# Attention values as the stationary operand, two heads on the two halves of the partitions, and router logits from rows not yet divided

## The chip, the cores and the metric

One core of a Trainium2 chip runs the whole kernel. The metric is device time in microseconds (us) of one execution, as the median of several runs. A smaller time is better.

## What is computed

Three stages follow each other. First a windowed attention over 4 batches, 8 heads, 576 positions and 64 values per head; each query sees itself and the 127 keys before it, with a bias that falls with the distance. Then a router sends each of the 2304 rows of 512 values to one of 8 experts. Last a gated layer with 1536 hidden units.

```python
scores = np.where(mask, scale * q @ k.T + bias, -1e9)      # mask: 0 <= query - key < 128
attn = exp(scores - max); attn = attn / (sum(attn) + 1e-9)
x = (attn @ v)                       # rows of 8 heads x 64 = 512 values
logits = x @ w_gate + modality_bias[modality_id]; e_idx = argmax(logits)
out = gate_w * (relu(x @ w1[e_idx]) @ w2[e_idx])
xn = out / rms * rms_g;  g = xn @ w_gate2;  return (g * sigmoid(g) * (xn @ w_val)) @ w_out
```

## The kernel before

The program is written in an order by hand: a list `AT` gives, for each half step n, the order of the routines and the lag of each. A query tile t has 128 rows; g = 0 and 1 are its two groups of four heads, so a tile has two half steps, and there are 18 tiles. A routine with lag L works in half step n on the pair (t, g) with 2t + g = n - L. Routines that work once for a tile run when g is 0. Each engine works through its own instructions in that order.

For one tile the routines are these. `tq`, `tk` turn the query and key rows on TensorE (bank "d", two buffers), and `qhi`, `khi` copy the result out on ScalarE. `qk` makes the scores (lag -1). It has queries stationary, 64 rows deep, and keys moving; the heads j = 0 and 1 of a pair lie on the two halves of the partitions. `ttr0`, `ttr1` add the bias on VectorE and find the largest. `exp0`, `exp1` make the exponentials on ScalarE with their sums. In the first six tiles `mix` and `pprev` fold the two key blocks on GpSimd. `pt` turns the weights on TensorE, `pall` (ScalarE) and `pcur` (VectorE) copy them out. `pv` (lag 2) multiplies by the values: the turned weights, 128 x 128, are stationary and 64 values of one head move, and the result in bank "c" (one buffer) has queries on partitions. A product of 32-bit operands appears as two LDWEIGHTS and two MATMUL records.

`xs` (lag 3, VectorE) divides that result by the sums and writes the row tile which is later sent away. `tx` (lag 4, TensorE) turns the row, `xhi` (lag 5, ScalarE) copies it out, `lg` (lag 6) multiplies by the 512 x 8 router weights into the bank "few", four products that accumulate into 8 columns. `gate` (lag 7, VectorE) adds the modality bias and finds the best expert, `gexp`, `rk` and `route` (lag 8) make the gate and the place of the row within its expert, and `place` (lag 9) sends the row to DRAM.

The bank "few" is one tile that also takes the counts of `rk` and the small turns of `mscale`. The latter makes a power of two from the largest of the weights, in five parts: part 0 on VectorE, part 1 a turn on TensorE (L598), part 2 on VectorE, part 3 two small products on TensorE (L603), part 4 on VectorE (L606 to L612). `SCALE` says in which half steps they start. Parts 1 and 3 stand ahead of `pt` of the next and the next but one half step, parts 2 and 4 at these half steps' ends.

While attention runs, the expert weights of the two experts chosen early are loaded (`weights`, on the SyncE queue with the loads of q, k and v and with the fills of DRAM) and split into high and low halves (`wsplits`, on ScalarE, GpSimd and VectorE, `SPLIT` pieces in a half step, and two a half step after the last entry of `SPLIT`). From half step 36 on, each half step ends with an eighth of the first expert product (`gemm1`), and after half step 44 `gemm2` follows, which needs all split pieces and their scaled copies (L637). All that comes later, from some 245 us on, is not touched.

Of the kernel before, what the change touches and what calls it, by code (L numbers as in the profile page):

```python
# [8 lines left out]
F32 = mybir.dt.float32  # L9
# [41 lines left out]
SPLIT = {**{n: 1 for n in range(25, 33)}, **{n: 2 for n in range(33, 37)}}  # L51
SCALE = {22: (0, 1), 25: (1, 2), 31: (2, 3), 36: (3, 4)}
# [31 lines left out]
def attn_moe_glu(tc, I, out, dbg=None):  # L84
    nc = tc.nc
    with contextlib.ExitStack() as top:
# [77 lines left out]
        wgn = tail.tile([P, KD, E], F32, name="wgn", bufs=1)  # L164
# [169 lines left out]
        def pv(t, g):  # L334
            full, oc, op = geo(t)[0], geo(t)[4], geo(t)[5]
            if g == 0:
                X[t] = bank("c", "xp").rearrange("p (h d) -> p h d", h=H)
            pa, pc = G.pop((t, g))[2:]
            for j in range(2):
                for u in range(2):  # L340
                    h = 4 * g + 2 * u + j
                    if mixed(t):
                        cur, prev = pc[:, j, u], pa[:, j, u]
                    else:
                        cur, prev = (pa, pc)[j][:, u, oc // P], (pa, pc)[j][:, u, op // P]
                    nc.tensor.matmul(X[t][:, h], cur, T["v", t][:, h], start=True, stop=not full)  # L346
                    if full:
                        nc.tensor.matmul(X[t][:, h], prev, T["v", t - 1][:, h], start=False, stop=True)  # L348
# [6 lines left out]
        def rs(t):  # L355
            r = small([P, H], F32, "rs")
# [4 lines left out]
        def xs(t):  # L361
            x = t1.tile([P, XW], F32, name=f"xs{t}") if t <= T0 else row_tile("xs")
            nc.vector.tensor_tensor(
                x[:, :D].rearrange("p (h d) -> p h d", h=H), X[t], M.pop(t)[:, :, None].to_broadcast([P, H, DH]), ALU.mult
            )
            X[t] = x

        def tx(t):
            x = bank("d", "tx")
            for k in range(KD):  # L370
                nc.tensor.transpose(x[:, k * P : k * P + P], X[t][:, k * P : k * P + P], ident)
            M[t] = x.rearrange("p (k x) -> p k x", k=KD)

        def xhi(t):
            x = block_tile("xT").rearrange("p (k x) -> p k x", k=KD)
            nc.scalar.activation(x, M[t], AF.Copy)
            M[t] = x

        def lg(t):
            x = M.pop(t)  # L380
            for k in range(KD):
                nc.tensor.matmul(few[:, P : P + E], x[:, k], wgn[:, k], start=k == 0, stop=k == KD - 1)  # L382
# [1253 lines left out]
```

## Time and profile before

| what | value |
| --- | --- |
| median of 3 runs | 866.93 us (861.96 to 879.2) |
| the profiled execution, its own time | 858.8 us |
| its span, first to last instruction | 857.1 us |
| attention, from the first turn of queries to the end of the last first-layer product | 4.8 to 224.4 us |
| mean granted clock of TensorE over the span | 0.975 of full speed |

The profile is of one execution. A matmul's recorded duration holds the time that its result needs to come out, so the distance from one start to the next tells more than the duration. Stretches named "tile" below run from the first query turn of one tile to that of the next.

### The profile page before, as it was taken

The page shows a single profiled execution, that of the slowest core. Times are in us where ns is not written, and L with a number is a line of the kernel's source. Part 1 is how long each engine was busy: PE and PEld are TensorE (multiplying, and loading weights), DVE is VectorE, ACT ScalarE, POOL GpSimd, SP SyncE. Part 2 cuts the span into 40 slices and gives each one's busy share as a digit, 9 for nine tenths or more (in the row PEclk, how much of TensorE's full clock was granted, in tenths as well). Part 3 has the DMA queues.
Part 4 walks back from the last instruction along what each step waited for, and adds up shares of the span by engine and source line. Part 5 has one row for each costly group of instructions (what it writes and reads, how often), then busy time and mean ns, then how long its engine had stood idle before and what let it go on. Part 6 is the DMA issues. An engine that isn't in the chain of part 4 may idle for free.

```text
span 857.1 us, 17524 instructions
## 1 busy us (share of the span) xinstructions
PE 815.1 (95%) x5826; PEld 560.2 (65%) x5826; DVE 610.2 (71%) x1685; ACT 433.9 (51%) x992; POOL 201.1 (23%) x259
## 2 busy tenths in 40 slices
PE   8999998989799999999999999899999999999994
PEld 6889787876345544444455555468787787888882
DVE  8778787875984578997676657667666676667752
ACT  6877777974544566774455433242333233233221
POOL 3552113575632234565100010000001001001001
PEclk9999997998899999999999999999999999999998
DMA  9974995652165655794652046001001000001001
GB/s 181 215 177 134 307 235 159 174 173 91 71 177 180 193 186 161 256 304 146 244 206 103 1 152 241 1 25 51 13 2 62 14 1 38 1 2 39 2 2 39
DMA packets 100473, 101.99 MB, mean 119 GB/s; under 512 B 63136, under 2 KB 75424, under 8 KB 100384
## 3 DMA queue, kind: packets, MB, share of 16 engines
q1 hardware_dynamic: 92848, 86.34, 35.0%
q0 software_dynamic: 4400, 14.20, 4.4%
q8 instruction: 53, 0.87, 0.4%
q10 hardware_dynamic: 3136, 0.30, 0.3%
q14 instruction: 36, 0.29, 0.1%
HBM read 67.18 MB, written 33.89 MB: 118 GB/s over the span
## 4 chain that ended last, share of the span: by engine, by line
issue 42%; PE 36%; DVE 10%; DMA 5%; ACT 4%; POOL 2%; SPq 0%; POOLq 0%; DVEq 0%; ACTq 0%
PE y L840 6%; PE h L807 6%; PE g L1184 4%; PE s L242 3%; PE xp L346 3%; PE xp L348 3%; PE pt L311 2%; PE acc L1359 2%; PE h L794 2%; DVE pb L270 1%; DMA raw<-gd 1%; ACT pb L281 1%; PE few L382 1%; DVE wr L777 1%; POOL out L863 1%
## 5 line engine op out<-in xcount | busy, mean ns | idle before, releaser
L1184 PE MATMUL g<-xc,gv 128*128 128x192 f16 x1680 | 146.7, 247 | 0.0
L1184 PEld LDWEIGHTS <-gv 128*128 128x128 f16 x1680 | 139.8, 98 | 9.3
L863 POOL DMA_INDIRECT out<-o,ix x18 | 17.8, 991 | 400.4 <-ACT o L1368 397.7
L840 PE MATMUL y<-W,wr 128*128 x304 | 91.9, 384 | 2.0 <-DVE fi L855 2.0
L840 PEld LDWEIGHTS <-wr 128*128 128x128 f16 x456 | 45.0, 99 | 61.6 <-issue 10.6
L1359 PE MATMUL acc<-go,alo 128*128 128x512 f16 x216 | 82.5, 382 | 0.0
L281 ACT ACTIVATE pb<-pb,mn 128x256 f32<-128x256 f32 (+4 forms) x160 | 74.5, 468 | 10.0 <-DVE mn L270 9.2
L1200 PE MATMUL gv<-xn,gv 128*128 128x384 f16 x432 | 75.1, 329 | 1.1 <-DVE one L1326 0.7
L1359 PEld LDWEIGHTS <-ahi 128*128 128x128 f16 x432 | 41.5, 98 | 41.6 <-issue 3.9
L807 PEld LDWEIGHTS <-W 128*128 x384 | 37.7, 99 | 44.4 <-issue 2.6
L1359 PE MATMUL acc<-go,ahi 128*128 128x512 f16 x216 | 64.3, 380 | 0.7 <-ACT ahi L1320 0.7
L897 POOL TENSOR_TENSOR cw<-cw,cv 128x512 int32<-128x512 int32 x36 | 50.2, 1394 | 62.9 <-issue 14.2
L840 PE MATMUL y<-wr,wr 128*128 x152 | 58.4, 384 | 5.4 <-DVE wr L637 5.4
L1200 PEld LDWEIGHTS <-gv 128*128 128x128 f16 x432 | 42.5, 98 | 31.9 <-issue 2.8
L270 DVE CUSTOM_DVE_ANT_0 pb<-s,bias 128x256 f32<-128x256 f32 (+4 forms) x160 | 53.5, 379 | 13.6 <-PE s L242 12.1
L807 PE MATMUL h<-xhi,W 128*128 128x512 f16 x192 | 59.3, 379 | 0.0
L1325 ACT ACTIVATE one<-one,undo 128x384 f32<-128x384 f32 x24 | 14.8, 615 | 83.1 <-DVE one L1316 83.1
L1359 PE MATMUL acc<-gv,ahi 128*128 128x512 f16 x180 | 54.2, 383 | 0.7 <-ACT ahi L1320 0.7
L1320 ACT ACTIVATE ahi<-one 128x384 f16<-128x384 f32 x36 | 18.8, 523 | 56.8 <-DVE one L1326 56.8
L242 PE MATMUL s<-kT,qT 64*128 64x256 f32 (+1 forms) x288 | 42.1, 403 | 0.6 <-DVE mn L270 0.4
L1316 DVE TENSOR_TENSOR u<-g,u 128x384 f32<-128x384 f32 x48 | 26.6, 555 | 17.0 <-PE g L1184 17.0
L1320 ACT ACTIVATE ahi<-other 128x384 f16<-128x384 f32 x36 | 18.8, 523 | 39.2 <-DVE other L1326 39.2
(331 smaller groups left out, 1768.0 us busy)
## 6 DMA issues: line engine op xcount, KB each, us to landing
raw<-gd SPq DMA_DIRECT2D x20, 768.0 KB, 4.5
gd<-cw SPq DMA_DIRECT2D x36, 256.0 KB, 3.3
wr<-in_moe_w SPq DMA_DIRECT2D x16, 512.0 KB, 6.0
cv<-in_moe_w_gate SPq DMA_DIRECT2D x12, 512.0 KB, 4.7
cv<-in_moe_w_val SPq DMA_DIRECT2D x12, 512.0 KB, 5.7
cv<-in_moe_w_out SPq DMA_DIRECT2D x12, 512.0 KB, 4.8
xd<-zrow SPq DMA_DIRECT2D x20, 257.0 KB, 4.9
xg<-xd SPq DMA_DIRECT2D x19, 257.0 KB, 3.2
```

Source lines behind the costliest of these rows:

```text
L242: nc.tensor.matmul(sps[j][:, u, :W], qT[rows, i], win(i, j), start=True, stop=True)
L270: nc.vector.tensor_tensor_reduce(pb[rw, u, x0:x1], sp[rw, u, x0:x1], bias[rw, h, b0 + x0 : b0 + x1], 1.0, 3.0e38, ALU.add, ALU.min, M[t][0 ...
L281: nc.scalar.activation(pb[rw, u, x0:x1], pb[rw, u, x0:x1], AF.Exp, bias=mn[rw, h : h + 1], scale=-1.0, accum_out=sm[rw, h : h + 1],)
L807: nc.tensor.matmul(hp, WH[0][k // 2][:, ds(w, 1), part, k % 2, q * P : q * P + P], x[:, k], start=k == 0 and n == 0, stop=k == KD - 1 and ...
L840: nc.tensor.matmul(y, x[:, k, cols], r, start=k == 0 and i == 0, stop=k == KF - 1 and i == 2)
L863: return nc.gpsimd.indirect_dma_start(dst[:, :], bass.IndirectOffsetOnAxis(ap=ix[:, 0:1], axis=0), src, None, bounds_check=NTOK - 1, oob_i ...
L897: nc.gpsimd.tensor_tensor(ci, ci, low.bitcast(I32), ALU.add)
L1184: nc.tensor.matmul(acc[:, gv * HT : gv * HT + HT], GV[p][:, a, gv, i, m * P : m * P + P], XC[c][:, b, j, m], start=m == 0 and n == 0, stop ...
L1200: nc.tensor.matmul(acc[:, :CHT], w[:, m * P : m * P + P], XC[c][b][:, k], start=k == 0 and n == 0, stop=k == KD - 1 and n == 2,)
L1316: add = lambda out, x, y: nc.vector.tensor_tensor(out, x, y, ALU.add)
L1320: nc.scalar.activation(ahi, si, AF.Copy, scale=2.0**-LOW)
L1359: nc.tensor.matmul(acc, a[:, cols], GO[f][part], start=f == 0 and n == 0, stop=f == NFF - 1 and n == 2,)
```

## The change

`pv` has the values (128 keys x 64) stationary and the turned weights (128 keys x 128 queries) moving. Heads j = 0 and 1 write to partitions 0 to 63 and 64 to 127 of the same columns, and their products alternate. The result has the 512 values on partitions and the queries along the columns. So `xhi` (now lag 4) copies it first, `tx` (lag 4, at the half step's end) turns it back into rows, and `lg` (lag 5) takes the undivided copy: for each k it multiplies by a 128 x 16 router block, two heads side by side with zeros in between, and writes 16 columns of its own, 64 in all. `xs` (lag 5) divides the turned rows. `gate` (lag 6) multiplies the 64 logits by 1/sum, adds over the heads (two VectorE instructions more), and goes on as before. Everything behind it has a lag smaller by one. `mscale` has all of its parts at the ends of half steps, `SCALE` and `SPLIT` start one half step earlier but for the last scale step, and the fills of DRAM come three instead of two in half steps 10 and 11, since they end one half step sooner.

```diff
-SPLIT = {**{n: 1 for n in range(25, 33)}, **{n: 2 for n in range(33, 37)}}
-SCALE = {22: (0, 1), 25: (1, 2), 31: (2, 3), 36: (3, 4)}
+SPLIT = {**{n: 1 for n in range(24, 32)}, **{n: 2 for n in range(32, 36)}}
+SCALE = {21: (0, 1), 24: (1, 2), 30: (2, 3), 36: (3, 4)}
...
-        wgn = tail.tile([P, KD, E], F32, name="wgn", bufs=1)
+        wgn = tail.tile([P, KD, 2 * E], F32, name="wgn", bufs=1)
...
-                X[t] = bank("c", "xp").rearrange("p (h d) -> p h d", h=H)
+                X[t] = bank("c", "xp").rearrange("p (k x) -> p k x", k=KD)
             pa, pc = G.pop((t, g))[2:]
-            for j in range(2):
-                for u in range(2):
-                    h = 4 * g + 2 * u + j
...
-                    nc.tensor.matmul(X[t][:, h], cur, T["v", t][:, h], start=True, stop=not full)
-                    if full:
-                        nc.tensor.matmul(X[t][:, h], prev, T["v", t - 1][:, h], start=False, stop=True)
+            for u in range(2):
+                for n in range(1 + full):
+                    for j in range(2):
+                        if mixed(t):
+                            p = (pc, pa)[n][:, j, u]
+                        else:
+                            p = (pa, pc)[j][:, u, (oc, op)[n] // P]
+                        i = 2 * g + u
+                        nc.tensor.matmul(
+                            X[t][DH * j : DH * j + DH, i], T["v", t - n][:, 2 * i + j], p, start=n == 0, stop=n == full
+                        )
...
+        def xhi(t):
+            x = block_tile("xT").rearrange("p (k x) -> p k x", k=KD)
+            nc.scalar.activation(x, X[t], AF.Copy)
+            X[t] = x
+
+        def tx(t):
+            x = bank("d", "tx")
+            for k in range(KD):
+                nc.tensor.transpose(x[:, k * P : k * P + P], X[t][:, k], ident)
+            X[t] = x, X[t]
+
+        def lg(t):
+            x = X[t][1]
+            for k in range(KD):
+                nc.tensor.matmul(few[:, P + 2 * E * k : P + 2 * E * (k + 1)], x[:, k], wgn[:, k], start=True, stop=True)
...
-            nc.vector.tensor_tensor_reduce(l, few[:, P : P + E], mbt, 1.0, 3.0e38, ALU.add, ALU.min, s[:, 0:1])
+            y = small([P, H, E], F32, "lh", 1)
+            nc.vector.tensor_tensor(
+                y, few[:, P : P + H * E].rearrange("p (h e) -> p h e", h=H),
+                M.pop(t)[:, :, None].to_broadcast([P, H, E]), ALU.mult,
+            )
+            nc.vector.tensor_reduce(l, y.rearrange("p h e -> p e h"), AX.X, ALU.add)
+            nc.vector.tensor_tensor_reduce(l, l, mbt, 1.0, 3.0e38, ALU.add, ALU.min, s[:, 0:1])
...
-            nc.scalar.activation(wgn, wg, AF.Copy, scale=-1.0)
+            nc.vector.memset(wgn, 0.0)
+            for j in range(2):
+                x = slice(DH * j, DH * j + DH)
+                nc.scalar.activation(wgn[x, :, E * j : E * j + E], wg[x], AF.Copy, scale=-1.0)
...
-            ("tq", -2), ("mix1", 1), ("gexp", 8), ("qhi", -2), ("rk", 8), ("xhi", 5), ("khi", -1), ("ttr0", 0),
-            ("ttr1", 0), ("lg", 6), ("ws", -1), ("exp0", 0), ("route", 8), ("weights", 11),
-            ("mix0", 0), ("tx", 4), ("pt", 1), ("pall", 1), ("exp1", 0), 
-            ("gate", 7), ("rs", 2), ("pv", 2), ("pprev", 1), ("qk", -1), ("xs", 3), ("vm", 1), ("place", 9), ("tk", -2),
+            ("tq", -2), ("mix1", 1), ("xhi", 4), ("gexp", 7), ("qhi", -2), ("rk", 7), ("khi", -1), ("ttr0", 0),
+            ("ttr1", 0), ("lg", 5), ("ws", -1), ("exp0", 0), ("route", 7), ("weights", 10), ("mix0", 0),
+            ("pt", 1), ("pall", 1), ("exp1", 0), ("gate", 6), ("rs", 2), ("pv", 2), ("pprev", 1),
+            ("qk", -1), ("xs", 5), ("vm", 1), ("place", 8), ("tk", -2), ("tx", 4),
             ("pcur", 1), ("wm", -1),
...
-                for x, r, w in fills[:2]:
+                m = 3 if 9 < n < FILL else 2
+                for x, r, w in fills[:m]:
...
-                if name == "pt":
-                    for x in (1, 2):
-                        if n - x in SCALE:
-                            mscale(*SCALE[n - x], 2 * x - 1)
...
-            for x, half in ((0, 0), (1, 2), (2, 4)):
+            for x, half in ((0, 0), (1, 1), (1, 2), (2, 3), (2, 4)):
                 if n - x in SCALE:
                     mscale(*SCALE[n - x], half)
```

## Rows read from the trace of the kernel before

**Rows 1.** The page's first part: busy us, share of the span, instructions, by engine.

```profile
PE 815.1 (95%) x5826; PEld 560.2 (65%) x5826; DVE 610.2 (71%) x1685; ACT 433.9 (51%) x992; POOL 201.1 (23%) x259
```

**Rows 2.** Stretches by tile: length, busy us by engine, granted clock, DMA share, GB/s.

```profile
core 0: us, PE busy (x) PEld busy (x) DVE busy (x) ACT busy (x) POOL busy (x), PEclk, DMA share, GB/s
...
27.80:36.70 8.90, 8.90 (x78) 8.04 (x76) 6.38 (x28) 6.84 (x22) 5.04 (x7) 1.00 0.94 214
36.70:47.00 10.30, 9.33 (x81) 8.17 (x79) 9.24 (x47) 9.42 (x32) 5.85 (x10) 1.00 0.77 197
...
66.40:76.40 10.00, 10.00 (x89) 9.05 (x87) 8.39 (x42) 7.64 (x27) 2.54 (x4) 1.00 0.52 132
76.40:85.90 9.50, 9.50 (x89) 8.86 (x87) 7.05 (x38) 6.80 (x23) 2.79 (x5) 1.00 0.50 145
...
95.00:106.90 11.90, 10.27 (x69) 8.26 (x67) 8.82 (x36) 8.13 (x28) 1.16 (x2) 0.86 1.07 298
...
128.60:145.80 17.20, 14.81 (x91) 12.81 (x90) 11.99 (x54) 11.84 (x38) 6.47 (x12) 0.70 0.47 135
145.80:156.40 10.60, 10.13 (x89) 9.07 (x87) 8.09 (x39) 10.50 (x36) 5.27 (x8) 1.00 0.67 179
156.40:166.30 9.90, 9.90 (x89) 9.01 (x87) 8.89 (x45) 8.84 (x28) 4.92 (x6) 1.00 0.69 187
...
188.00:201.40 13.40, 11.16 (x52) 8.68 (x51) 7.00 (x18) 5.13 (x13) 7.32 (x11) 0.62 0.06 21
...
224.40:234.40 10.00, 4.64 (x14) 1.65 (x13) 9.93 (x21) 3.64 (x7) 7.63 (x7) 0.66 0.07 27
```

**Rows 3.** Timeline of TensorE's matmuls over one half step: start, length, line, count.

```profile
152.60 1.04 PE L311 MATMUL pt<-ident,pb 128*128 128x128 f32 x8
153.47 0.33 PE L346 MATMUL xp<-vn,pa 128*128 128x64 f32 x2
...
154.76 0.39 PE L346 MATMUL xp<-vn,pc 128*128 128x64 f32 x2
154.98 0.39 PE L348 MATMUL xp<-vn,pc 128*128 128x64 f32 x2
155.30 1.14 PE L242 MATMUL s<-kT,qT 64*128 64x256 f32 x8
156.36 0.66 PE L187 MATMUL tq<-ident,qn 128*128 128x128 f32 x4
```

**Rows 4.** Lines L348 and L598, weight loads and matmuls: ns min/median/max, starts, shape.

```profile
L348 PEld LDWEIGHTS xp<-vn,pa x168: 191/193/334, 21.2 to 202.1; 128*128 128x128 f32 x168
L348 PE MATMUL xp<-vn,pa x168: 274/275/422, 21.3 to 202.2; 128*128 128x64 f32 x168
...
L598 PEld LDWEIGHTS few<-ident,mam x4: 79/80/84, 113.1 to 201.1; 128*1 128x1 f32 x4
```

**Rows 5.** Timeline of two engines around a scale step.

```profile
130.07 0.63 PE L371 MATMUL tx<-ident,xs 128*128 128x128 f32 x4
...
132.86 0.17 DVE L420 TENSOR_TENSOR ranks<-few,ranks 128x16 f32<-128x16 f32 x1
...
133.09 0.37 PE L598 MATMUL few<-ident,mam 128*1 128x128 f32 x1 [2.39 <-DVE ranks L420]
```

**Rows 6.** Who waited for whom, 0 to 220 us: total us, times, longest.

```profile
DVE xs L363 <- PE xp L348: 10.3, 12, 1.2
...
DVE l L389 <- PE few L598: 6.5, 1, 6.5
...
DVE vmax L351 <- DMA vn<-in_v: 2.5, 1, 2.5
```

**Rows 7.** VectorE's instructions by line, 76.4 to 85.9 us: busy us, mean ns.

```profile
L351 DVE TENSOR_REDUCE vmax<-vn 128x1 f32<-128x512 f32 x1 | 0.7, 677 | 0.0
...
L420 DVE TENSOR_TENSOR ranks<-few,ranks 128x16 f32<-128x16 f32 x1 | 0.2, 155 | 0.0
```

**Rows 8.** Timeline of TensorE where the second expert product starts.

```profile
230.35 0.59 PE L840 MATMUL y<-wr,wr 128*128 x1 [5.36 <-DVE wr L637]
```

More of the change, by code (lines that the diff above doesn't have):

```diff
@@ L336, in pv @@
             if g == 0:
-                X[t] = bank("c", "xp").rearrange("p (h d) -> p h d", h=H)
+                X[t] = bank("c", "xp").rearrange("p (k x) -> p k x", k=KD)
             pa, pc = G.pop((t, g))[2:]
-            for j in range(2):
-                for u in range(2):
-                    h = 4 * g + 2 * u + j
[L342 to L345, printed above, removed]
-                    nc.tensor.matmul(X[t][:, h], cur, T["v", t][:, h], start=True, stop=not full)
-                    if full:
-                        nc.tensor.matmul(X[t][:, h], prev, T["v", t - 1][:, h], start=False, stop=True)
+            for u in range(2):
[9 more added lines that the diff above has]
+                        )
         def vm(t):
@@ L355, in rs @@
         def rs(t):
-            r = small([P, H], F32, "rs")
+            r = small([P, H], F32, "rs", 3)
             nc.vector.tensor_scalar(r, M.pop(t)[1], 1e-9, None, ALU.add)
@@ L359, in rs @@
             M[t] = r
[L361 to L365, printed above, removed]
+        def xhi(t):
+            x = block_tile("xT").rearrange("p (k x) -> p k x", k=KD)
+            nc.scalar.activation(x, X[t], AF.Copy)
             X[t] = x
@@ L370, in tx, with xs @@
             for k in range(KD):
[L371 to L377, printed above, removed]
+                nc.tensor.transpose(x[:, k * P : k * P + P], X[t][:, k], ident)
+            X[t] = x, X[t]
         def lg(t):
-            x = M.pop(t)
+            x = X[t][1]
             for k in range(KD):
-                nc.tensor.matmul(few[:, P : P + E], x[:, k], wgn[:, k], start=k == 0, stop=k == KD - 1)
+                nc.tensor.matmul(few[:, P + 2 * E * k : P + 2 * E * (k + 1)], x[:, k], wgn[:, k], start=True, stop=True)
+        def xs(t):
+            x = t1.tile([P, XW], F32, name=f"xs{t}") if t <= T0 else row_tile("xs")
+            nc.vector.tensor_tensor(
+                x[:, :D].rearrange("p (h d) -> p h d", h=H), X[t][0].rearrange("p (h d) -> p h d", h=H),
+                M[t][:, :, None].to_broadcast([P, H, DH]), ALU.mult,
+            )
+            X[t] = x
         def gate(t):
@@ L388, in gate @@
             mbt = MB[:, t] if t < NT - 2 else MBL[:, t - NT + 2]
-            nc.vector.tensor_tensor_reduce(l, few[:, P : P + E], mbt, 1.0, 3.0e38, ALU.add, ALU.min, s[:, 0:1])
+            y = small([P, H, E], F32, "lh", 1)
+            nc.vector.tensor_tensor(
+                y, few[:, P : P + H * E].rearrange("p (h e) -> p h e", h=H),
+                M.pop(t)[:, :, None].to_broadcast([P, H, E]), ALU.mult,
+            )
+            nc.vector.tensor_reduce(l, y.rearrange("p h e -> p e h"), AX.X, ALU.add)
+            nc.vector.tensor_tensor_reduce(l, l, mbt, 1.0, 3.0e38, ALU.add, ALU.min, s[:, 0:1])
             k8 = small([P, E], F32, "k8")
@@ L948, in attention_step @@
             if 3 <= n < 2 * T0 + LAG["route"] + 1 or n >= FILL:
-                for x, r, w in fills[:2]:
+                m = 3 if 9 < n < FILL else 2
+                for x, r, w in fills[:m]:
                     nc.sync.dma_start(x[r : r + P], (EX[1] if EX else zrow)[:, :w])
-                fills = fills[2:]
+                fills = fills[m:]
+                assert n < FILL - 1 or all(x is yd for x, _, _ in fills)
             for name, lag in AT:
```

## The prediction

> **What bounds the kernel now.** I read the page's totals first. TensorE is busy for 815.1 of 857.1 us and VectorE for 610.2 [rows 1], but such shares mix stages, so I cut the attention at each tile's first query turn [rows 2]. The reader is to compare, in each row, TensorE's busy time with the length and then with the next busiest engine. From 66.40 to 76.40 and from 76.40 to 85.90 TensorE is busy without a break, and VectorE has 8.39 and 7.05 us of work. Here TensorE sets the pace. In the tile from 36.70 TensorE has 9.33, ScalarE 9.42 and VectorE 9.24 of 10.30 us, so relief of one alone gives little. In the one from 145.80 ScalarE fills 10.50 of 10.60. From 95.00 on the DMA engines are full (1.07) and VectorE waits 2.5 us for a load of values [rows 6]. The tile from 128.60 takes 17.20 us at a mean clock of 0.70. The nine other stretches of attention repeat these patterns; their numbers are in the sum below as gains only.
>
> Then the timeline, for what a half step costs on TensorE [rows 3]. Two records of `pv` start every 154.98 - 154.76 = 0.22 us, so one takes 0.11 us, although only 64 columns move. A load of the 128 columns of weights stands before each. That the load is the limit is read from the neighbour: eight turns of 128 columns take 153.47 - 152.60 = 0.87 us, 0.11 each, with twice the moving columns. A full half step has 16 such records: 16 x 0.112 = 1.79 us. From the last pair of `pv` to `qk` it is 155.30 - 154.98 = 0.32 instead of 0.22: 0.1 us is lost on the change to products 64 rows deep. `qk` takes 156.36 - 155.30 = 1.06 us for four pairs of records.
>
> Last the waits. At 133.09 the turn of a scale step had idled TensorE for 2.39 us until `route` (L420) had read the bank "few" at 132.86 [rows 5]. After it the clock is at 1.2 instead of 2.4 GHz for most of the tile [rows 2]. A later scale step keeps VectorE from `gate` (L389) for 6.5 us [rows 6].
>
> **The change part by part.** *`pv`.* The 16 records remain, but each streams 128 columns from a 64-column load, and two heads use different halves of the array's columns. No row shows two column halves. The nearest row is `qk`, whose heads use two halves of the array's rows: four pairs of 256 columns in 1.06 us, of which 0.2 goes to entering and leaving, so (1.06 - 0.2) / 4 = 0.215 us for a pair, 0.108 for a pair of 128 columns [rows 3]. If the column halves run side by side as these row halves do, a half step has 8 pairs x 0.11 = 0.88 us. If they take turns it is 16 x 0.11 = 1.76. I take the first, since `qk` is the same pattern of 32-bit products with j alternating. The loads go on under the stream: a 128-column load lasts 191 ns, a one-column load 79 [rows 4], so a 64-column load lies between, and now the load of 128 columns fits into each 0.11 us.
>
> The Trainium skill, page "TensorEngine Tiling (Array Packing)", section "When to Use Tiling", recommends just this swap with two column tiles when 64 columns move, up to twice as fast; the trace before has no such product, so no row confirms it.
>
> One more change of the array's shape per half step, from turns to `pv`, costs 0.1 to enter and 0.1 for the first load that nothing covers, 0.2 us by the same rows (bounds: nothing, if the change into `qk` replaces it, and 0.4). So a full half step of TensorE saves 1.79 - 0.88 - 0.2 = 0.71 us, a tile 1.4. Over 32 full and 4 short half steps (0.25 each) that is 23.7 us if nothing else were in the way.
>
> *What the records meet.* `gate` grows by a product and a sum of 64 elements on VectorE. A 16-element operation takes 155 ns and a 512-element reduction 677 [rows 7]; two of 64 lie between 0.3 and 1.4 us, and I take 0.45, near the first, per tile. It gives something back: `xs` waited 10.3 us in 12 tiles for `pv` of its own half step [rows 6], and now reads a turn made in the half step before. `xhi` stands near the head of ScalarE's half step, before `gexp`, `qhi`, `khi` and the exponentials, and waits for `pv` of the half step before. `pv` ends a whole `qk`, 1.06 us, before that half step does, so I cost the wait at nothing; without that cover ScalarE would lose up to 1 us a tile. `tx` moves from the middle of TensorE's half step to its end, ahead of nothing that is due; it needs `xhi`, 0.6 us into the half step. `lg` moves 16 columns instead of 8 under the same loads: nothing. The second copy and the clearing of the router block are once and early: nothing, below 1 us with no cover. On SyncE the third fill (257 KB) stands before loads in two half steps; at the 197 to 214 GB/s of that stretch [rows 2] it is 1.3 us of DMA, which the loads' lead covers.
>
> So a tile's new length is the largest of TensorE less 1.4, VectorE plus 0.45 and ScalarE, with 0.3 for waits that don't overlap. The tile from 66.40 goes from 10.0 to 9.0, the one from 76.40 from 9.5 to 8.4. With the two beside them (one held by VectorE) I count 3.2 us. The tile from 27.80 has its DMA engines at 0.94, so it can't fall below 8.4, a gain of 0.5; the one before it 0.3, the one from 36.70 0.4, the next 0.7. The tile from 95.00 gains nothing and the next 0.2, since the weights' loads fill the DMA engines. The tile from 145.80 gains nothing (ScalarE), the one from 156.40 goes to 8.89 + 0.45 + 0.3, a gain of 0.3, the last one 1.3. The two stretches around the first product (from 176.4 and 201.4) gain 0.7 each for their `pv`. Together 8.3.
>
> *The scale steps.* At a half step's end the turn's read of "few" lies a whole half step behind, so the 2.39 us go. VectorE's part 2 now waits at the half step's end for part 1, which lies behind `qk`. What is queued behind it is `ttr0`, which needs that `qk` anyway. In the tile from 128.60 the stall goes and so should the slow clock: a mean of 0.70 over 17.2 us means 10.3 us at half speed, 5.1 us of loss. I count 2.4 + 4.9 = 7.3 there, and 1.2 for the smaller stalls at 117 to 128.6.
>
> *The end of attention.* From 188.00 to 201.40 the clock averages 0.62 [rows 2], 10.2 us at half speed or 5.1 lost. Fewer waits may keep it up; I count half, 2.5, and 0.7 for `pv`. At 230.35 TensorE had idled 5.36 us for the last scaled copies of the second weights [rows 8], and the clock over that stretch averages 0.66, so 6.8 of its 10 us lie at half speed and 3.4 are lost. The splits start one half step earlier and VectorE's 6.5 us behind the scale step shrink, so I count 2.5 of the gap and 1.0 of the 3.4 us of clock. Next late there is VectorE itself, busy 9.93 of 10.0 us [rows 2], which is why I don't count all. Together 6.7.
>
> The sum is 8.3 + 7.3 + 1.2 + 6.7 = 23.5 us. Against the profiled execution: 858.8 - 23.5 = 835.3. The median of the runs is 866.9, 8.1 above that execution, and I take it that the new kernel's runs lie as its did: 866.9 - 23.5 = 843.
>
> **The rivals.** *The next engine takes it all.* The halves run side by side, but ScalarE, VectorE and the loads hold every tile. For it speaks that three engines are above 9.2 us in the tile from 36.70, against it the rows from 66.40 and 76.40. Then what remains is the scale step and part of the end, about 10 us: 857.
>
> *The halves take turns*, so the change doesn't do what it says. `pv` stays at 1.76 us and the change of shape adds 0.2 to each of 36 half steps, of which some 60% is on the path: +4. The scale step gives 7.3 back: 864. For it: column halves are in no row.
>
> *The loads are bare, and the kernel is slower.* The place is `pv`. If loads for one half can't go in while the other streams and the halves take turns too, a record costs its stream, 0.108, and a 64-column load, half of the 0.11 of a 128-column one: 0.163 us. 544 records then take 89 us instead of 61, with the changes of shape +35; the scale and end steps return some 14: 888. The rival decides above a pair's cost where 272 pairs and 7 us of changes exceed 61 us and the 14 us back: 0.25 us a pair. Against it: in `pv` now, loads of 191 ns stand under matmuls that started before them, since records follow every 0.112 us [rows 3, 4]. The Trainium skill, page "TensorE: Matmul & The Clock Gate", section "Part 3: Packing small matmuls — row/col tiling", says that a weight load overlaps matmuls in flight only when their row groups differ. By that rule the two column halves, which share all rows, would give this rival's time. The rows of `pv` speak against the rule as it stands, since there load and matmul use the same 128 rows.
>
> **How the numbers follow.** My forecast has 0.60, all engines held 0.16, turns 0.11, bare loads 0.08. A better case has 0.05: both slow stretches of the clock go and the gap at 230 too, 826. Faster by over 2% means below 849.6, about what a measurement of this kernel can tell from no change. The forecast's own range is 830 to 854 (0 to 0.4 us for the change of shape is 14 us at most, half of it on the path; the clock's parts are 5 us either way). It lies below 849.6 in nine cases of ten: 0.54, with the better case and the edge of the second rival 0.58. Slower has the bare loads, 0.08. The rest, 0.34, is within 2%. The range from 825 to 861 leaves out the turns and the bare loads, 0.19 together.
>
> **What would show it.** The timeline: `pv` records that start two by two, pairs every 0.11 us, 1.1 us from `pt`'s end to `qk` instead of 1.8. By tile: 8.4 to 9.0 us from 66 to 86, with VectorE near 90% busy. No idle time before L598 on TensorE, and the clock at its upper level in what was 128.6 to 145.8. `xs` not in the list of waits. At the second product, a gap below 3 us. I am wrong if the pairs lie 0.2 us or more apart, if ScalarE or VectorE waits appear at every `xhi`, or if a thinner TensorE falls to the lower clock in tiles where it is now at the upper one: one such tile costs 5 us, as the one from 128.60 does.

## The result, and the profile after

The changed kernel takes 842.15 us (median of 4 runs, 838.5 to 846.15), the kernel before took 864.98 us beside it (4 runs, 861.96 to 879.2). The ratio is 0.9745, with a 95% interval of 0.9691 to 0.9799: faster, and close to the predicted 843. The profiled execution of the new kernel is its slowest one, 846.15 us, where that of before (858.8) was below its median. The pair of profiles therefore shows 12.7 of the 22.8 us, and the splits of many executions further down are needed for the rest.

The page of the changed kernel, to be held against [rows 1]: busy us, share and instructions by engine, and the granted clock in 40 slices.

```profile
span 844.4 us, 17545 instructions
...
PE 796.0 (94%) x5826; PEld 527.2 (62%) x5826; DVE 622.8 (74%) x1722; ACT 434.4 (51%) x993; POOL 201.4 (24%) x259
...
PEclk9999897999899999999999999999999999999998
```

TensorE has the same 5826 matmuls and is busy 19.1 us less. VectorE is busy 12.6 us more. Two slices of slow clock remain in attention, and one where the second product starts.

TensorE's timeline in the changed kernel: one half step, which answers to [rows 3]; then the places around 94, 130, 156 and 215 us.

```profile
76.75 1.04 PE L311 MATMUL pt<-ident,pb 128*128 128x128 f32 x8
77.72 0.32 PE L347 MATMUL xp<-pa,vn 128*64 128x128 f32 x1
77.73 0.32 PE L347 MATMUL xp<-pc,vn 128*64 128x128 f32 x1
...
78.10 0.27 PE L347 MATMUL xp<-pa,vn 128*64 128x128 f32 x1
78.10 0.27 PE L347 MATMUL xp<-pc,vn 128*64 128x128 f32 x1
78.21 0.27 PE L347 MATMUL xp<-pa,vn 128*64 128x128 f32 x1
...
78.54 0.27 PE L347 MATMUL xp<-pc,vn 128*64 128x128 f32 x1
78.74 1.13 PE L242 MATMUL s<-kT,qT 64*128 64x256 f32 x8
...
97.55 0.66 PE L311 MATMUL pt<-ident,pb 128*128 128x128 f32 x2 [3.11 <-DVE pc L326]
...
129.81 0.67 PE L242 MATMUL s<-kT,qT 64*128 64x256 f32 x2 [1.29 <-DVE mn L270]
131.26 2.04 PE L242 MATMUL s<-kT,qT 64*128 64x256 f32 x6 [0.78 <-DVE mn L270]
...
156.16 0.70 PE L242 MATMUL s<-kT,qT 64*128 64x256 f32 x2 [2.20 <-DVE mn L270]
...
215.24 0.38 PE L851 MATMUL y<-wr,wr 128*128 x1 [3.05 <-DVE wr L648]
...
217.41 0.59 PE L851 MATMUL y<-wr,wr 128*128 x1 [0.72 <-DVE wr L648]
```

`pv` records start two by two, one for each half of the columns, and a pair every 78.21 - 78.10 = 0.11 us. From the first to `qk` it is 78.74 - 77.72 = 1.02 us, where it was 155.30 - 153.47 = 1.83 [rows 3]. The weight loads of that line, to be held against [rows 4], last 137 ns each, longer than the 0.11 us in which two of them go in:

```profile
L347 PEld LDWEIGHTS xp<-pa,vn x272: 132/137/232, 13.3 to 191.1; 128*64 128x64 f32 x136
```

Stretches by tile in the changed kernel, columns as in [rows 2]. In order they answer to the tiles from 27.80, 36.70, 56.90, 66.40, 76.40, 95.00, 128.60, 145.80 and 156.40 there; the last two rows are the start of the second product and the slow stretch of the clock in it.

```profile
28.50:36.40 7.90, 7.76 (x80) 6.18 (x78) 7.39 (x31) 6.31 (x22) 4.28 (x6) 1.00 1.06 228
36.40:47.00 10.60, 9.34 (x80) 6.79 (x78) 9.84 (x48) 10.15 (x36) 6.74 (x11) 1.00 0.71 188
...
56.20:67.00 10.80, 9.22 (x84) 6.88 (x82) 10.14 (x54) 6.51 (x22) 3.37 (x6) 1.00 0.58 115
67.00:76.20 9.20, 8.71 (x88) 7.06 (x86) 8.71 (x47) 7.63 (x26) 2.13 (x3) 1.00 0.56 151
76.20:84.30 8.10, 8.10 (x88) 6.91 (x86) 6.45 (x34) 6.97 (x24) 3.01 (x6) 1.00 0.78 235
93.50:107.40 13.90, 10.78 (x68) 8.10 (x66) 10.73 (x43) 9.59 (x30) 1.17 (x2) 0.75 1.07 258
125.90:142.50 16.60, 14.28 (x89) 11.32 (x88) 13.41 (x61) 14.52 (x46) 7.07 (x12) 0.69 0.39 97
142.50:151.00 8.50, 8.50 (x88) 7.08 (x86) 8.26 (x33) 7.72 (x25) 4.64 (x9) 1.00 0.95 250
151.00:162.90 11.90, 9.56 (x89) 7.37 (x88) 11.38 (x51) 8.94 (x29) 5.31 (x8) 1.00 0.62 168
...
211.50:221.50 10.00, 6.23 (x20) 2.20 (x18) 9.66 (x29) 2.54 (x5) 5.54 (x5) 0.75 0.01 2
216.50:223.30 6.80, 6.08 (x15) 2.02 (x14) 6.21 (x34) 0.00 (x0) 0.71 (x1) 0.51 0.01 2
```

The row of the kernel before that answers to the one from 56.20, which [rows 2] leave out:

```profile
56.90:66.40 9.50, 9.50 (x85) 8.61 (x83) 8.73 (x48) 6.47 (x20) 2.29 (x4) 1.00 0.68 163
```

Two tiles that TensorE held became shorter: 10.0 to 9.2 and 9.5 to 8.1. So did the one that ScalarE filled, 10.6 to 8.5. In 36.40 ScalarE (10.15) and VectorE (9.84) are the long ones. The tile from 56.20, where TensorE had been busy without a break, grew from 9.5 to 10.8 us, and VectorE now has 10.14 of them. In 151.00 VectorE has 11.38 of 11.90. The tiles from 93.50 and 151.00 grew by 2.0 us each, and the one from 125.90 is still at a mean clock of 0.69.

The waits of the changed kernel, 0 to 220 us, as in [rows 6]: total, times, longest.

```profile
ACT pb L281 <- DVE mn L270: 13.5, 11, 2.8
...
PE s L242 <- DVE mn L270: 6.1, 5, 2.2
...
DVE vmax L352 <- DMA vn<-in_v: 4.4, 2, 2.7
```

`xs` is gone from that list. The long waits of ScalarE and TensorE here are for VectorE (the additions of the bias, L270; ScalarE's were 9.2 us in the kernel before), and VectorE waits for the values that `vm` (L352) reads.

VectorE's lines in the changed kernel, 19 to 173 us, columns as in [rows 7], then its timeline at 153 with GpSimd's:

```profile
L380 DVE TENSOR_TENSOR xs<-tx,rs 128x512 f32<-128x512 f32 x15 | 10.2, 681 | 0.0
...
L396 DVE TENSOR_REDUCE l<-lh 128x8 f32<-128x64 f32 x14 | 3.8, 268 | 0.5
...
L392 DVE TENSOR_TENSOR lh<-few,rs 128x64 f32<-128x64 f32 x14 | 3.1, 219 | 0.1
```
```profile
152.90 0.17 DVE L708 TENSOR_SCALAR counts<-counts 128x2 f32<-128x2 f32 x1
...
153.24 0.95 DVE L711 TENSOR_SCALAR tabt<-rowA,counts 128x4 f32<-128x4 f32 x1
153.47 0.69 POOL L642 TENSOR_SCALAR wr<-wr,mup 128x512 f32<-128x512 f32 x1
154.23 1.19 DVE L712 SCALAR_TENSOR_TENSOR base<-rowB,counts,tabt 128x4 int32<-128x4 f32 x1
154.25 1.15 POOL L643 TENSOR_TENSOR W<-wr,W 128x512 f16<-128x512 f32 x1
155.34 0.41 DVE L270 CUSTOM_DVE_ANT_0 pb<-s,bias 128x256 f32<-128x256 f32 x1
```

The two instructions added to `gate` take 219 and 268 ns, 18 x 0.49 = 8.8 us of VectorE's 12.6. At 153 two four-column operations of the table of chosen experts take 0.95 and 1.19 us ahead of the bias additions that the exponentials wait for. Each ends within 0.03 us of the GpSimd instruction beside it. TensorE's idle 2.20 us at 156.16 stand right behind them.

**Where the time went, by place.** Start times of the first instruction of a kind, in the two profiled executions:

| stretch | before | after | gained | forecast |
| --- | --- | --- | --- | --- |
| to the end of the last query-turn tile | 176.4 | 172.9 | 3.5 | 15.4 |
| from there to the first product `h` | 21.0 | 13.7 | 7.3 | 3.9 |
| first `h` to the first `y` | 26.9 | 24.9 | 2.0 | 0.7 |
| first `y` to the last matmul | 621.3 | 620.8 | 0.5 | 3.5 |

The gap of [rows 8] lies behind the first `y`, so its 3.5 us of forecast stand in the last row.

**Work and clock, over all executions.** Span times mean granted clock gives an estimate of what the span would be at the upper clock; the remainder is lost to the clock. It is exact only where TensorE sets the pace: a low clock while TensorE stands idle counts as lost here, though it costs nothing. For the profiled pair: 857.1 x 0.975 = 835.7 with 21.4 lost, and 844.4 x 0.980 = 827.5 with 16.9 lost. Medians over the executions of each kernel; slow executions, over 1.5% above the fastest of their kernel, are left out of the last two columns. Those of the first row come from the 25 executions of the kernel before that were run beside the experiments, with a median time of 862.58 us:

| kernel | time, us | at the upper clock | lost to the clock |
| --- | --- | --- | --- |
| before | 864.98 | 837.2 | 24.9 |
| changed | 842.15 | 823.2 | 17.3 |
| scale_ends | 851.28 | 837.5 | 11.0 |
| no_swap | 848.21 | 835.0 | 12.7 |
| swap_only | 845.20 | 831.0 | 12.7 |
| oldscale | 847.07 | 828.4 | 17.3 |
| late_splits | 847.54 | 829.3 | 16.9 |
| turns | 846.53 | 834.9 | 9.3 |
| vm2_before | 879.17 | 842.0 | 35.5 |
| vm2_after | 848.05 | 831.3 | 14.8 |
| vm_short | 839.06 | 821.3 | 15.1 |
| vm_lag2 | 840.19 | 822.2 | 16.3 |
| v_early | 835.49 | 825.5 | 8.3 |
| v_early_act | 839.86 | 824.8 | 14.7 |

The experiments were run in three sets. The kernel before comes to 839.1 us of work and 21.5 us of clock beside turns, scale_ends, oldscale and vm2_after, to 835.9 and 25.0 beside vm2_before, vm_short, vm_lag2 and late_splits, and to 837.3 and 25.0 beside the others. Differences of some 3 us between kernels of different sets are therefore not told apart.

So the change is worth about 14 us of work (837.2 to 823.2) and 8 us of clock. The prediction had 15.1 and 8.4. Its total and this division held; its places did not.

### The profile page after: what moved, and what is told of

It reads as the page before. It is cut to its first block, busy times and chain, and to the rows that moved or that the text cites. A ratio compares the mean times of both kernels' runs of the same rounds, so it can differ in the third digit from the quotient of the medians.

```text
span 844.4 us, 17545 instructions
## 1 busy us (share of the span) xinstructions
PE 796.0 (94%) x5826; PEld 527.2 (62%) x5826; DVE 622.8 (74%) x1722; ACT 434.4 (51%) x993; POOL 201.4 (24%) x259
## 4 chain that ended last, share of the span: by engine, by line
issue 43%; PE 28%; DVE 19%; DMA 4%; ACT 4%; POOL 1%; SPq 0%; POOLq 0%; DVEq 0%; ACTq 0%
PE y L851 9%; PE h L818 5%; PE g L1193 4%; DVE pb L270 4%; PE acc L1368 2%; PE s L242 2%; PE h L805 2%; DVE wr L788 1%; PE xp L347 1%; POOL out L874 1%; ACT pb L281 1%; DVE wmax L906 1%; DMA vn<-in_v 1%; DVE pc L326 1%; DVE wr L648 1%
## 5 line engine op out<-in xcount | busy, mean ns | idle before, releaser
L851 PE MATMUL y<-W,wr 128*128 x304 | 93.8, 391 | 2.2 <-DVE fi L866 2.2
L1334 ACT ACTIVATE one<-one,undo 128x384 f32<-128x384 f32 x24 | 14.8, 615 | 83.1 <-DVE one L1325 83.1
L270 DVE CUSTOM_DVE_ANT_0 pb<-s,bias 128x256 f32<-128x256 f32 (+4 forms) x160 | 53.3, 378 | 3.8 <-PE s L242 2.2
L242 PE MATMUL s<-kT,qT 64*128 64x256 f32 (+1 forms) x288 | 47.1, 406 | 6.6 <-DVE mn L270 6.1
L242 PEld LDWEIGHTS s<-kT,qT 64*128 64x128 f32 x288 | 28.7, 192 | 17.9 <-DVE mn L270 7.0
L1325 DVE TENSOR_TENSOR u<-g,u 128x384 f32<-128x384 f32 x48 | 26.6, 555 | 16.9 <-PE g L1193 16.9
```

The costliest lines, as they stand in the source:

```text
L242: nc.tensor.matmul(sps[j][:, u, :W], qT[rows, i], win(i, j), start=True, stop=True)
L270: nc.vector.tensor_tensor_reduce(pb[rw, u, x0:x1], sp[rw, u, x0:x1], bias[rw, h, b0 + x0 : b0 + x1], 1.0, 3.0e38, ALU.add, ALU.min, M[t][0 ...
L851: nc.tensor.matmul(y, x[:, k, cols], r, start=k == 0 and i == 0, stop=k == KF - 1 and i == 2)
L1325: add = lambda out, x, y: nc.vector.tensor_tensor(out, x, y, ALU.add)
```

## The experiments

The theory to be tested was that of the prediction: the column halves run side by side, and what TensorE saves is cut off by the next engine; the scale steps give their stall and a slow clock on top. The rivals were that one part alone gives everything, and that VectorE, not TensorE, is what counts. Ratios are to the kernel before, run beside each set of kernels (medians of 862.58 to 870.39 us there), with 95% intervals.

**turns: one half of the columns after the other.** The order of `pv`'s loops alone:

```diff
-            for u in range(2):
-                for n in range(1 + full):
-                    for j in range(2):
+            for j in range(2):
+                for u in range(2):
+                    for n in range(1 + full):
```

> The changed kernel, but the products of one head group stand one behind the other (head j outermost), so that neighbours use the same half of the array's columns and the halves can't run side by side. Theory TensorE: the gain comes from the halves running together and TensorE sets the pace in most of attention; a full half step costs 0.8 us more on TensorE, 32 of them, some 60% on the path: 15 us slower than the changed kernel's 842, about 857. Rival VectorE: after the change VectorE and the loads set the pace nearly everywhere, so most of the 0.8 us a half step is slack: within 5 us of 842. Either way the records of the two halves should no longer start together.

846.53 us (844.27 to 849.1), ratio 0.9808 (0.9766 to 0.985). TensorE's timeline of this kernel, same half step:

```profile
77.25 0.76 PE L347 MATMUL xp<-pa,vn 128*64 128x128 f32 x5
77.74 0.32 PE L347 MATMUL xp<-pc,vn 128*64 128x128 f32 x1
77.84 0.27 PE L347 MATMUL xp<-pa,vn 128*64 128x128 f32 x1
...
78.12 0.71 PE L347 MATMUL xp<-pc,vn 128*64 128x128 f32 x5
...
78.76 1.13 PE L242 MATMUL s<-kT,qT 64*128 64x256 f32 x8
```

Five `pa` records start alone. The halves then overlap in the middle all the same, although the program has all eight `pa` records first. `pv` takes 78.76 - 77.25 = 1.51 instead of 1.02 us, and so in nearly every other full half step of the two traces. That is 0.49 us for a half step, 15.7 us for the 32 full ones. In the table, 834.9 - 823.2 = 11.7 us of it show in the span at the upper clock, so by this estimate TensorE's `pv` is on the path for about three quarters. The time rose by only 4.4 us. That is what the rival with VectorE expected, and not the 15 us of the theory. By the table the difference lies in the clock, of which less is lost: 7.6 to 12.7 us in the six executions here, 13.4 to 17.7 in the four of the changed kernel. The kernel with the busier TensorE kept its clock better. If that is the cause, a part of what a shorter `pv` saves is handed back; that it is the cause, and not where the stalls happen to fall, is not shown.

**scale_ends and oldscale: the scale steps alone, and the change without them.** In scale_ends the kernel before takes this edit; in oldscale the changed kernel takes it backwards:

```diff
-                if name == "pt":
-                    for x in (1, 2):
-                        if n - x in SCALE:
-                            mscale(*SCALE[n - x], 2 * x - 1)
...
-            for x, half in ((0, 0), (1, 2), (2, 4)):
+            for x, half in ((0, 0), (1, 1), (1, 2), (2, 3), (2, 4)):
```

> The kernel before with the scale steps' parts at the half steps' ends, and nothing else of the change (their half steps as before). Theory of the forecast: the 2.39 us stall at 130.7 and the slow clock behind it go, 7 us off 865, 858, and VectorE's 6.5 us wait near 195 shrinks. Rival: VectorE waits at the half step's end for the turn, and the clock falls anyway: 862 to 866, no change that can be measured.

> The changed kernel with parts 1 and 3 of the scale steps put back ahead of the turns of the weights, all else as changed. Theory of the forecast: the stall before the turn L609 comes back (up to 2.4 us at two of the steps) and a slow stretch of the clock with it, 5 to 8 us slower than 842, 847 to 850. Rival: the changed kernel's profile shows the slow stretch at 131.2 us all the same, set off by waits for VectorE, so the moved parts bring only the stall itself: 842 to 845.

scale_ends: 851.28 us (846.91 to 859.86), ratio 0.9866 (0.981 to 0.9922). oldscale: 847.07 us (843.87 to 847.98), ratio 0.9807 (0.9765 to 0.9848). The tiles of scale_ends that answer to the ones from 128.60 and 145.80 in [rows 2], and its scale turn, which answers to [rows 5]:

```profile
126.30:138.40 12.10, 11.20 (x91) 9.68 (x89) 11.31 (x54) 11.73 (x37) 6.42 (x12) 1.00 0.80 228
138.40:150.90 12.50, 11.70 (x88) 10.73 (x87) 8.43 (x40) 10.50 (x36) 5.27 (x8) 0.86 0.43 132
```
```profile
132.48 0.27 PE L598 MATMUL few<-ident,mam 128*1 128x128 f32 x1
...
139.91 0.17 PE L408 MATMUL few<-oh,upper 128*128 128x8 bf16 x1 [0.80 <-DVE mam L606]
```

The turn no longer waits and the clock stays up in this tile: 17.2 us became 12.1. ScalarE now has 11.73 us of them and VectorE 11.31. But TensorE then waits 0.80 us for the end of the scale step (L606), the clock falls in the next tile (0.86), and that tile takes 12.5 us instead of 10.6. The two together went from 27.8 to 24.6, a gain of 3.2 us where the prediction had 7.3. The kernel as a whole gained more than the 7 us expected of it. Over all executions next to nothing of the gain is work (837.2 to 837.5, or from 839.1 in its own set) and the rest is clock (24.9 to 11.0, or from 21.5). In the changed kernel the same step is worth the other kind: without it 828.4 - 823.2 = 5.2 us more work, and no difference in clock (17.3 in both). So the step holds, and by this estimate what it pays in depends on what lies around it.

**no_swap and swap_only: each half of the change by itself.** no_swap is scale_ends with the new `SPLIT` and `SCALE`; swap_only is oldscale with the old ones. What is called the swap here is the product together with its shorter chain and the fills; these were not taken apart.

```diff
-SPLIT = {**{n: 1 for n in range(25, 33)}, **{n: 2 for n in range(33, 37)}}
-SCALE = {22: (0, 1), 25: (1, 2), 31: (2, 3), 36: (3, 4)}
+SPLIT = {**{n: 1 for n in range(24, 32)}, **{n: 2 for n in range(32, 36)}}
+SCALE = {21: (0, 1), 24: (1, 2), 30: (2, 3), 36: (3, 4)}
```

> The kernel before with the scale steps at the half steps' ends and one half step earlier, and the splits one half step earlier, as in the changed kernel: all of the change but the swapped product with its shorter chain. The scale steps' place alone gave 12 us (863 to 851), and the splits' later start cost the changed kernel 5. Theory swap (forecast): the swapped product is worth 8 us of the 22, so 849 to 852. Rival steps: the scale steps and splits are nearly all of the gain, 863 - 12 - 5, 843 to 847.

> The changed kernel with the scale steps and the splits as they were before, in place and half step: the swapped product with its shorter chain alone. Theory swap: 8 us or more off 863, 850 to 855. Rival steps: the stalls at the scale steps and the late splits take all of it, 859 to 863.

no_swap: 848.21 us (841.66 to 852.4), ratio 0.9809 (0.974 to 0.9879). swap_only: 845.2 us (844.07 to 846.99), ratio 0.9779 (0.9725 to 0.9833). Either half gives most of the gain, 1.9% and 2.2%, and both together 2.55%, not 4.1%. The three intervals overlap. In work the swap is worth 837.2 - 831.0 = 6.2 us by itself and 835.0 - 823.2 = 11.8 us once scale steps and splits are early. In clock each half alone loses 12.7 us, both together 17.3; single executions overlap (5.9 to 15.3, 11.8 to 16.0, and 13.4 to 17.7).

**late_splits: the changed kernel with `SPLIT` as before.** The first line of that diff, taken back alone.

> The changed kernel with the splits of the expert weights in the half steps of before (one later). Theory of the forecast's last term: the earlier start made the gap before the second expert product smaller (5.36 before, 3.05 after), so 2 to 4 us come back there, 844 to 846. Rival: the gap is set by VectorE's and ScalarE's work after the first product starts, and the start of the splits doesn't matter: 841 to 843.

847.54 us (844.41 to 857.62), ratio 0.9825 (0.9761 to 0.989): 829.3 - 823.2 = 6.1 us of work come back, more than expected. Without the swap the early splits were worth less, 837.5 - 835.0 = 2.5 us from scale_ends to no_swap. The prediction counted them only in the gap before the second product, at 2.5 us. That gap did grow, from 3.05 to 6.68 us:

```profile
217.89 0.59 PE L851 MATMUL y<-wr,wr 128*128 x1 [6.68 <-DVE wr L648]
```

Where the rest of the 6.1 us lies was not located.

**vm2_after and vm2_before: more work for VectorE.** Both kernels get a second 512-element reduction in each tile, 18 x 0.68 = 12.2 us:

```diff
             nc.vector.tensor_reduce(
                 vmax[:, t : t + 1], T["v", t].rearrange("p h d -> p (h d)"), AX.X, ALU.max, apply_absolute_value=True
             )
+            nc.vector.tensor_reduce(vextra, T["v", t].rearrange("p h d -> p (h d)"), AX.X, ALU.max, apply_absolute_value=True)
```

> The changed kernel with one more reduction of 512 values of V on VectorE in each tile, written to a place that nobody reads: 0.68 us of VectorE per tile, 12 us over 18 tiles. Theory TensorE: VectorE has slack, 0 to 3 us slower than 842. Rival VectorE: it sets the pace in 10 to 14 of the tiles, 7 to 10 us slower, 849 to 852.

> The kernel before with the same one more reduction of 512 values on VectorE in each tile, 0.68 us, read by nobody. If TensorE set the pace before the change, as its rows from 66 to 86 us showed, this is hidden in most tiles: 0 to 4 us slower than 865. If VectorE already did, 7 to 10 us slower.

vm2_after: 848.05 us (843.36 to 850.82), ratio 0.9824 (0.9778 to 0.987). vm2_before: 879.17 us (872.08 to 882.21), ratio 1.0178 (1.012 to 1.0235). In the changed kernel 8.1 of the 12.2 us show as work (831.3 - 823.2). In the kernel before only 4.8 do (6.1 in its own set), but 10.6 us more are lost to the clock (35.5 - 24.9). One place where TensorE waits for the reading of "few" on VectorE, in that kernel's waits from 100 to 220 us; without the addition the longest of these waits was the 2.39 us of [rows 5]:

```profile
PE few L600 <- DVE ranks L422: 4.8, 2, 3.0
```

The old kernel's 16.6 us lie above what either theory expected, so VectorE was near the path already. In work the changed kernel pays more for the addition, in time the old one does (879.17 - 862.58 = 16.6 us against 848.05 - 842.15 = 5.9). That the change moved VectorE closer to the path is therefore not shown.

**vm_short: less work for VectorE.** The changed kernel's reduction reads 8 values instead of 512, so the true largest value of V is left out.

```diff
-                vmax[:, t : t + 1], T["v", t].rearrange("p h d -> p (h d)"), AX.X, ALU.max, apply_absolute_value=True
+                vmax[:, t : t + 1], T["v", t][:, 0, :8], AX.X, ALU.max, apply_absolute_value=True
```

> The changed kernel with the reduction over V's 512 values cut to 8 values, so that the largest value of V is not found over all (this part is left out): 0.5 us less on VectorE per tile, 9 us over 18 tiles. Rival VectorE: it sets the pace after the change, 5 to 8 us faster than 842, 834 to 837. Theory TensorE: no change, 840 to 843.

839.06 us (837.14 to 840.59), ratio 0.9718 (0.967 to 0.9766). Taking some 9 us off gives 1.9 us of work (823.2 - 821.3), which is within what the sets differ by, and its interval overlaps that of the changed kernel. Adding to VectorE costs two thirds, taking off gives a fifth at most. That the engines are level and another is next at once fits this, but which one it is was not shown.

**vm_lag2, v_early, v_early_act: the wait for the values.** In vm_lag2 `vm` stands a half step later. In v_early the values are loaded two half steps earlier into a fourth buffer. v_early_act adds to v_early that `pcur` copies on ScalarE for g = 1 in tiles 6 to 10; in the six tiles before them `pcur` goes another way.

```diff
-            ("qk", -1), ("xs", 5), ("vm", 1), ("place", 8), ("tk", -2), ("tx", 4),
+            ("qk", -1), ("xs", 5), ("vm", 2), ("place", 8), ("tk", -2), ("tx", 4),
```
```diff
-                x = a2.tile([P, H, DH], F32, name=src + "n", tag=src + "n", bufs=3 if src == "v" else 2)
+                x = a2.tile([P, H, DH], F32, name=src + "n", tag=src + "n", bufs=4 if src == "v" else 2)
...
-            if n % 2 == 0 and 2 <= n < 2 * NT:
-                load(n // 2, "v")
+            if n % 2 == 0 and 0 <= n < 2 * NT - 2:
+                load(n // 2 + 1, "v")
```
```diff
-                nc.vector.tensor_copy(pc[:, :, :nb], G[t, g][1][:, :, :nb])
+                if g == 1 and t < 11:
+                    nc.scalar.activation(pc[:, :, :nb], G[t, g][1][:, :, :nb], AF.Copy)
+                else:
+                    nc.vector.tensor_copy(pc[:, :, :nb], G[t, g][1][:, :, :nb])
```

> The changed kernel with the reduction over V one half step later, in the even half steps, so that VectorE doesn't stand waiting for the load of V that was issued a half step before. VectorE's wait of 2.7 us near 94 us and TensorE's 3.1 us behind it should go, and with them perhaps a slow stretch of the clock of 6.8 us (3.4 us lost): 836 to 840. Rival: the product with V then waits for the same load itself, and the even half steps, which hold the gate, become the longer ones on VectorE: 841 to 845.

> The changed kernel with four instead of three buffers for V and each V tile loaded two half steps earlier. If VectorE's wait for V near 94 us, TensorE's 3.1 us idle behind it and the slow clock that follows (6.8 us, 3.4 us lost) come from the load's short lead, all go: 836 to 839. If the weights' loads fill the DMA engines so that any load is late there, the stall moves to the queries' or keys' load: 841 to 843.

> As the last, and in the tiles 6 to 10 the second half step's copy of the turned weights goes from VectorE to ScalarE (0.68 us of VectorE less per tile, 0.6 us of ScalarE more). If VectorE sets the pace in these tiles, where it has 8.4 to 10.1 us of work and ScalarE 6.5 to 7.6, each gets 0.3 to 0.6 us shorter: 2 to 3 us below the run with the early loads alone. If TensorE sets it, no difference.

vm_lag2: 840.19 us (836.54 to 842.67), ratio 0.9728 (0.9677 to 0.9779). v_early: 835.49 us (833.12 to 844.59), ratio 0.9697 (0.9627 to 0.9767). v_early_act: 839.86 us (834.01 to 843.79), ratio 0.9702 (0.9635 to 0.9769). ScalarE's and then TensorE's timeline of vm_lag2 at the place where TensorE stood for 3.11 us in the changed kernel, and TensorE's in v_early:

```profile
97.78 1.06 ACT L598 ACTIVATE W<-wr 128x1024 bf16<-128x1024 f32 x1 [2.27 <-DMA wr<-in_moe_w]
...
98.84 0.58 ACT L364 ACTIVATE xT<-xp 128x512 f32<-128x512 f32 x1
```
```profile
99.47 0.32 PE L347 MATMUL xp<-pa,vn 128*64 128x128 f32 x1 [3.07 <-ACT xT L364]
```
```profile
95.30 0.32 PE L347 MATMUL xp<-pa,vn 128*64 128x128 f32 x1 [2.15 <-ACT xT L364]
```

The stall did not go, it changed hands: ScalarE now stands for the weights' load, `xhi` (L364) is queued behind it, bank "c" is not free, and `pv` waits. v_early is the fastest kernel here; its gain is clock (8.3 against 17.3 lost, in single executions 5.0 to 17.7), not work (825.5). Its interval overlaps that of the changed kernel, as vm_lag2's does. Moving `pcur` brought nothing more. What sets off each of the remaining slow stretches of the clock stays open.

## Why the prediction was right, and where its steps were not

*`pv`: right.* The forecast took the side-by-side case, 0.88 + 0.2 = 1.08 us for a half step; it is 1.02, with pairs every 0.11 us. Where the halves are kept apart it is 1.51 us, although TensorE then still overlaps a part. The two rivals that cost more fall with this: bare loads would have put pairs at 0.33 us. The Trainium skill, page "TensorE: Matmul & The Clock Gate", section "Part 3: Packing small matmuls — row/col tiling", makes the overlap of a load with matmuls in flight depend on different row groups. These loads share all rows, two of 137 ns go into each 0.11 us, and none shows as a gap, so here the measurement decides against it. The Trainium skill, page "TensorEngine Tiling (Array Packing)", section "Theoretical Speedup", has up to twice the speed for a dimension of 64; the trace agrees, with 1.83 / 1.02 = 1.8.

*How much of TensorE's saving reaches the end: right in size.* 8.3 + 0.7 = 9.0 us of the 23.7 us of `pv` were counted. The swap measured 6.2 us by itself and 11.8 on top of the rest, by the estimate of work. That it needs the earlier steps to get there was not seen.

*The tiles: right in the two worked out, wrong by up to 2.3 us elsewhere, and by more in the one from 128.60.* 9.0 and 8.4 were forecast for the tiles from 66.40 and 76.40, 9.2 and 8.1 came. The one from 56.90 is one of the two beside them and lost 1.3 us, with VectorE as the long engine. The one from 145.80 was put at no gain because of ScalarE's 10.50 us, and gained 2.1: ScalarE has 7.72 us there now and 14.52 in the tile ahead, 22.24 together where it had 11.84 + 10.50 = 22.34. The same work fell on the other side of the cut, so one tile's 10.50 was no floor. The ones from 95.00 and 156.40 lost 2.0 us each where 0 and 0.3 of gain stood in the sum. In the latter, 1.5 us are the two table operations, which took 0.43 and 0.22 us in the kernel before.

*VectorE's additions: right in size.* 0.219 + 0.268 = 0.49 us against 0.45, and the waits of `xs` went. "Here TensorE sets the pace" was said of two tiles, and it does not hold for the whole of attention: 12.2 us more on VectorE cost the old kernel 4.8 + 10.6 = 15.4 us, work and clock.

*"In the tile from 128.60 the stall goes and so should the slow clock": the step that failed in its place.* Its stall went. In the changed kernel the clock falls at 131 all the same (mean 0.69), now after 1.29 and 0.78 us in which TensorE waited for the bias additions. The tile gained 0.6 us, and with the next one 27.8 became 25.1, a gain of 2.7 instead of 7.3. The 7.3 us could hardly have come at any clock: the forecast leaves the two tiles 27.8 - 7.3 = 20.5 us, and ScalarE alone has 22.34 us of work in them [rows 2]. The prediction's own rule, that a tile's length is that of its busiest engine, was not applied to this sum. The scale steps by themselves bring 3.2 us there, as scale_ends shows. In the changed kernel the clock came back elsewhere: from 176.4 to the first `h` 7.3 us were gained where 3.9 were counted, since the slow stretch from 188.00 [rows 2] is gone. The sum of the clock terms, 8.4 us, met the measured 7.6 (24.9 - 17.3). As the places differ, that agreement is partly luck. So is that of the total: by places the profiled pair gained 13.3 us of the 23.5, in part because the profiled execution of the changed kernel has 827.5 us of work, above its median of 823.2.

*The end of attention: the gap right, its worth wrong.* The gap before the second product was put at 5.36 - 2.5 = 2.9 us and is 3.05; VectorE is busy 9.66 of 10.0 us there, as it was. But 2.5 + 1.0 us were counted for it, and from the first `y` on only 0.5 came. In the changed kernel TensorE stops a second time (0.72 us at 217.41), and the clock is at 0.51 from 216.50 to 223.30, under matmuls. In the kernel before, 6.8 us at half speed lay in the 10 us from 224.40 [rows 2]; the matmuls went on only at 230.35 [rows 8], so at least 6.8 - 4.05 = 2.75 us of them fell into idle time and cost nothing. The 3.4 us that the prediction called lost there were at most 2.0.

*"I cost the wait at nothing" (`xhi` behind `pv`): right as it was meant, but the wait the other way round was not listed.* No wait of ScalarE for `pv` shows before `xhi` in the changed kernel. But `pv` of the next tile needs bank "c" back, which `xhi` reads, and on ScalarE `xhi` stands behind the search for the largest weight (L598), which waits for the weights' load. In vm_lag2 and v_early, where VectorE no longer waits for the values, TensorE stands 3.07 and 2.15 us for it. The prediction has no term for this.

*The rival of engines that take it all* describes the tiles from 36.70 and 56.90, but not the sum: the measured 842 is 15 us below its 857.

## What to carry to other kernels

Forecast work and clock as separate sums: span times mean granted clock over several executions is an estimate that tells them apart, and here an edit of a scale step paid almost wholly in clock in one kernel and wholly in work in the other. Before a slow stretch is counted as a gain, see what the other engines have to do in it, over two tiles and not one, and whether TensorE was idle in it anyway. When the busiest engine gets shorter, list for each stage who is second and what in its queue stands ahead of the instruction that matters; where the loads fill the DMA engines, a stall that was taken from one engine came back at another that waits for a load. An improvement on TensorE was worth more here once the other engines' late work had been moved earlier, so the parts of such a change should be tried together and singly.

## What the hardware showed that was not expected

- Two column halves of the array took 64-column loads of 137 ns each and 128-column streams at a pair every 0.11 us, with no load visible.
- In the trace TensorE did not keep strictly to the program's order between the halves: in turns, `pc` records start at 77.74 while three of the eight `pa` records are still to come.
- A kernel with 0.49 us more of TensorE's work in each half step lost less to the clock, 9.3 against 17.3 us in the median, with no overlap between the executions.
- Operations of 128 x 4 elements on VectorE took 0.95 and 1.19 us at 153 in the changed kernel, where each ended with the GpSimd instruction beside it, and 0.43 and 0.22 us in the kernel before. The 128 x 8 operation of L399 in `gate` shows the same over the whole trace of the changed kernel: 0.23 us in each of the eight cases without a GpSimd instruction beside it, and 0.80 to 1.21 us in the five beside a TENSOR_TENSOR of GpSimd. No run moves the GpSimd work away to test it.
